# Inverse square root chains of a fused LayerNorm, long-convolution and mixer kernel on GpSimd, with a newly searched issue order

## The chip, the cores and the metric

The kernel runs on one core of a Trainium2 chip. The metric is the device time of one execution in microseconds. Within the core five engines work side by side, each through its own instructions in order: PE (TensorE, matrix products; PEld is its weight load), DVE (VectorE), ACT (ScalarE), POOL (GpSimd) and SP (SyncE, which here only issues DMA transfers). An engine that has to wait holds up everything behind it in its own queue.

## The reference

With S = 2048 positions and D = 512 channels, all in bf16, and `ln` a LayerNorm without weights:

```python
def _layernorm(x, axis=-1, eps=1e-5):
    m = jnp.mean(x, axis=axis, keepdims=True)
    v = jnp.var(x, axis=axis, keepdims=True)
    return (x - m) / jnp.sqrt(v + eps)
...
def _A_ref(q, k, v, shift_k, ssm_k, ssm_D):
    ...                                # k_shift: four shifted copies of k, weighted by shift_k
    kv = k_shift * v
    ...                                # y: causal convolution of kv with ssm_k along S, by FFT
    y = y + kv * ssm_D[None, None, :]
    return q * y
def _B_ref(x, w1, w2, w3, w4):
    h = _gelu(_layernorm(x, axis=-1) @ w1)
    ...                                # g0..g3: quarters of h, shifted by 1, -1, 2, -2 positions
    hs = jnp.concatenate([g0, g1, g2, g3], axis=-1) @ w2
    x1 = x + hs
    h2 = _gelu(_layernorm(x1, axis=-1) @ w3) @ w4      # w3: 512 x 1792, w4: 1792 x 512
    return x1 + h2
x = A_q
h = x + _A_ref(_layernorm(x), A_k, A_v, A_shift_k, A_ssm_k, A_ssm_D)
return h + _B_ref(_layernorm(h), B_w1, B_w2, B_w3, B_w4)
```

Three LayerNorms follow each other: of q, of h, and inside B of the normalised h and then of x1. Each needs an inverse square root of a variance per position.

## The kernel before

**Tiles.** The 2048 positions are 16 tiles `t` of 128 positions; groups `b` = 0 to 3 hold four tiles each. Pairs of tiles are `u` = 0 to 7 (`t` = 2u and 2u+1).

**Stages.** First k is transposed and shifted on PE (`pk`, `psh`), and the convolution runs as two levels of a discrete Fourier transform: `stage_a` makes PSUM tiles `pah` and `pak`, `stage_c` makes `pc`. `product` multiplies the spectra on DVE (L674) and adds the parts (L688, L690). The way back begins with `pg` (L744). Every one of these PSUM tiles has to be evicted to SBUF, by `evac` (L171 on ACT, L173 on DVE).

The h stage follows. `last_level(u)` ends the inverse transform on PE into a PSUM tile `py` (two tiles wide); two instructions scale it by the inverse deviation of q and add 1 (`scaled`, L805 on ACT, L807 on DVE). `gate(u)` multiplies by the centred q on DVE (L812), which is h, and takes the statistics of both tiles (`stats`: bn_stats L620, aggregate L621). When two pairs of a group are there, `rsqrt_h(b)` computes the inverse deviations with all their by-products: two additions to the variance (L824, L825), a first guess by integer arithmetic (L601), two Newton steps of three instructions each (L603 to L605), the negative mean times the factor (`nb`, L827) and a residual weight `rho` (L832, L833). `norm_h(b, i)` then normalises each tile (`hn`, L840 on ACT, L843 on DVE). The normalised tiles are transposed into `xT`: those of b = 0 and 1 by PE (`pt2`, L856, evicted through L171), those of b = 2 and 3 by transposing DMAs on SP's queue (L900).

Then come the products. `gelu_mm("w1", …)` (`pw`, L868; GELU on ACT, L872) makes the hidden state `gT`. `mix(b)` takes shifted columns of `gT` times w2 (`p2`, L945), adds the residual on DVE (`x1`, L951), takes statistics, runs the same inverse square root chain for x1 (L959, L601 to L605, L961), normalises (`xnorm`, L969 on ACT, L972 on DVE), and transposes (PE for b = 0, SP's DMAs, L978, for the rest). Last, for each group, `pw` with w3 and GELU, the product with w4 (`p4`, L1014), the final addition (L1019) and the store. `of` (L1000) prepares the residual.

**Fills.** `warm_up` and `keep` (L880, tile `pv`) are matmuls of zeros that nothing reads.

**The chain.** `newton` yields the seven instructions of guess and Newton steps; `chain` adds each of them to the plan as an operation of DVE of its own. All chains are on DVE; GpSimd has nothing to do behind the front.

**The order.** Nothing is issued when it is called. Each step is recorded in a `Plan` with what it reads and writes and the engines that it may run on. `ISSUE`, a long list of operation numbers that a search left and that is written out in the kernel, then says in which order all of them go to their engines; a letter behind a number (A, V) chooses between ACT and DVE. Costs such as `{"V": 0.58}` or `lat` go into that search alone; they have no effect on the program. Within each engine the list's order is the order of execution.

What the list before says around the h stage: PE runs `pw` of b = 0 and 1, `p2` of t = 4 and 2, `pw` of b = 2, a fill, `p2` of t = 6, `pw` of b = 3, `p2` of t = 8. The eviction of py of u = 0 is shared, one half on DVE and one on ACT; all others are on ACT. SP's eight transposes are t = 8, 11, 10, 9, 15, 14, 12, 13.

## Time and profile before

| | us |
|---|---|
| device time, median of 3 runs | 243.62 (242.0 to 243.78) |
| device time of the profiled execution | 243.34 |
| its span | 241.5 |
| PE busy in the span | 224.7 |
| DVE busy | 161.0 |
| ACT busy | 153.1 |
| POOL busy | 15.4 |

The profile is one execution, recorded instruction by instruction. Its views are a page with the busy time of each engine and the costliest groups of instructions; a timeline; groups of instructions by line within a window; windows with each engine's busy time; and the chain of waits, which is followed back from the last instruction, at each step to what released it, or to the instruction before it on its engine. A line of a group reads: line, engine, operation, tiles, shapes, count, then busy time and mean duration in ns, then the idle time of the engine just before and what ended it. Durations of one DVE, ACT or POOL instruction contain a tail that overlaps with the next one, so that how far an engine advances is read from start to start.

### The profile page before, as it was taken

Reading aid. Unit: us, or ns where it says so; the run is one execution under the profiler, and the core shown is the slowest. Engines: PE = TensorE matmul, PEld = TensorE weight load, DVE = VectorE, ACT = ScalarE, POOL = GpSimd, SP = SyncE. Lnnn points to the kernel's source line nnn. Section 1 sums busy time; section 2 is a strip of 40 time slices with the busy share of each in tenths; the row PEclk is TensorE's granted clock in tenths of the full one; section 3 lists DMA queues with packets and bytes.
Section 4 is the critical chain, followed back from the end, with each engine's and each line's share of the span. In section 5 each row is a group of like instructions: output and inputs, shape, how many; then the busy total and the mean of one; then the engine's idle time right before and its main releaser. Section 6 shows DMA issues by size and latency. Waiting matters only on the chain.

```text
span 241.5 us, 5031 instructions
## 1 busy us (share of the span) xinstructions
PE 224.7 (93%) x2069; PEld 147.6 (61%) x2069; DVE 161.0 (67%) x380; ACT 153.1 (63%) x205; POOL 15.4 (6%) x30
## 2 busy tenths in 40 slices
PE   8899987998899977999969999999999999999994
PEld 7899987897799864574434544444444444444454
DVE  6954999999999997999998899910440044004421
ACT  5788769999979998889657399763036204630000
POOL 2359300000000000000000000000000000000000
PEclk9999999999999999999999999999999999999999
DMA  6998876740000099100640025320002012001111
GB/s 218 391 374 203 168 187 213 174 91 3 0 3 0 20 343 390 39 0 0 88 84 5 1 53 99 61 52 3 10 22 54 0 24 65 0 0 42 46 43 45
DMA packets 22182, 21.82 MB, mean 90 GB/s; under 512 B 11916, under 2 KB 18704, under 8 KB 22160
## 3 DMA queue, kind: packets, MB, share of 16 engines
q1 hardware_dynamic: 21904, 21.37, 32.7%
q8 instruction: 16, 0.26, 0.5%
q10 hardware_dynamic: 256, 0.14, 0.2%
q14 instruction: 6, 0.05, 0.1%
HBM read 13.11 MB, written 2.10 MB: 63 GB/s over the span
## 4 chain that ended last, share of the span: by engine, by line
PE 51%; DVE 25%; DMA 12%; ACT 6%; issue 2%; SPq 1%; DVEq 0%; ACTq 0%
PE pw L868 23%; PE p L1014 20%; DVE kin L674 6%; DMA kin<-in_A_v_dram 5%; PE p L945 4%; DVE bst L620 4%; DVE ab L173 4%; ACT s L171 3%; DMA q_sb<-in_A_q_dram 3%; ACT ab L171 3%; DMA kin<-in_A_k_dram 2%; DVE ab L812 2%; DMA act<-ab 2%; DVE kin L688 1%; DVE bst L624 1%
## 5 line engine op out<-in xcount | busy, mean ns | idle before, releaser
L868 PE MATMUL pw<-act,wts 128*128 128x512 bf16 x288 | 64.0, 379 | 2.5 <-DMA act<-ab 1.9
L872 ACT ACTIVATE ab<-pw 128x512 bf16<-128x512 f32 x56 | 33.0, 596 | 38.4 <-PE pw L868 27.3
L1019 DVE TENSOR_TENSOR wts<-p,wts 128x1024 bf16<-128x1024 f32 (+2 forms) x10 | 10.1, 1012 | 62.0 <-PE p L1014 62.0
L868 PEld LDWEIGHTS <-wts 128*128 128x128 bf16 x288 | 28.0, 98 | 36.3 <-DMA act<-ab 2.4
L1014 PE MATMUL p<-wts,ab 128*128 128x512 bf16 (+1 forms) x238 | 48.9, 366 | 0.0
L1014 PEld LDWEIGHTS <-ab 128*128 128x128 bf16 x238 | 23.3, 98 | 25.3
L542 PE MATMUL pc<-ab,Wc 128*128 128x256 bf16 x128 | 30.7, 282 | 1.4 <-DVE ab L173 1.1
L171 ACT CAST s<-pc 128x1024 bf16<-128x1024 f32 x31 | 29.6, 1044 | 1.4 <-DVE kin L674 1.3
L544 PE MATMUL pc<-ab,Wc 128*128 128x128 bf16 x128 | 29.0, 227 | 0.0
L543 PE MATMUL pc<-ab,Wc 128*128 128x128 bf16 x128 | 28.0, 219 | 0.0
L543 PEld LDWEIGHTS <-Wc 128*128 128x128 bf16 x128 | 19.4, 151 | 1.4 <-issue 1.4
L674 DVE TENSOR_TENSOR kin<-s 128x2048 bf16<-128x2048 bf16 x16 | 19.4, 1221 | 0.6
L542 PEld LDWEIGHTS <-Wc 128*128 128x128 bf16 x128 | 19.4, 151 | 0.3
L544 PEld LDWEIGHTS <-Wc 128*128 128x128 bf16 x128 | 18.2, 142 | 0.0
L477 PE MATMUL psh<-ab 128*128 128x128 bf16 x256 | 15.6, 219 | 0.4 <-DVE kvq L481 0.4
L171 ACT CAST ab<-pah 128x1024 bf16<-128x1024 f32 x13 | 12.8, 1023 | 4.8 <-PE pah L518 4.8
L477 PEld LDWEIGHTS <-ab 128*128 128x128 bf16 x256 | 14.4, 98 | 0.9 <-issue 0.4
L945 PE MATMUL p<-wts,act 128*128 128x512 bf16 x64 | 15.0, 379 | 0.0
L481 DVE TENSOR_TENSOR kvq<-psh,kin 128x1024 bf16<-128x1024 f32 x8 | 9.7, 1218 | 4.8 <-DMA kin<-in_A_v_dram 4.8
L171 ACT CAST ab<-pak 128x1024 bf16<-128x1024 f32 x13 | 12.5, 1061 | 0.0
L951 DVE SCALAR_TENSOR_TENSOR s<-ab,rho,p 128x512 bf16<-128x512 bf16 x16 | 11.5, 739 | 1.2 <-PE p L945 1.1
L1000 DVE SCALAR_TENSOR_TENSOR wts<-s,mq,ab 128x512 f32<-128x512 bf16 x16 | 11.2, 749 | 0.2
(139 smaller groups left out, 316.3 us busy)
## 6 DMA issues: line engine op xcount, KB each, us to landing
wts<-in_B_w_dram SPq DMA_DIRECT2D x2, 1792.0 KB, 11.1
kin<-in_A_k_dram SPq DMA_DIRECT2D x4, 512.0 KB, 5.8
ab<-in_A_ssm_k_dram SPq DMA_DIRECT2D x4, 512.0 KB, 8.6
kin<-in_A_v_dram SPq DMA_DIRECT2D x4, 512.0 KB, 13.6
q_sb<-in_A_q_dram SPq DMA_DIRECT2D x8, 256.0 KB, 6.1
kin<-kvq SPq DMA_DIRECT2D x16, 128.0 KB, 5.1
out_dram<-wts SPq DMA_DIRECT2D x14, 128.0 KB, 2.3
Wc<-ab SPq DMA_DIRECT2D x4, 384.0 KB, 5.3
```

Of the source, the lines that this page charges most:

```text
L171: A.copy(o, src)
L477: T_.matmul(pv[:, g, i, :], lhsT=row(g, 4 * qr + i - j), rhs=dg()[:, 2 * g + cc, j, :], start=(j == 0), stop=(j == 3))
L542: T_.matmul(pv[:, kk], lhsT=W[0], rhs=T[:, :, 2 * k1:2 * k1 + 2, :], start=True, stop=False)
L543: T_.matmul(pv[:, kk, :, 0, :], lhsT=W[1], rhs=T[:, :, 2 * k1 + 1, :], start=False, stop=False)
L544: T_.matmul(pv[:, kk, :, 1, :], lhsT=W[2], rhs=T[:, :, 2 * k1, :], start=False, stop=True)
L674: v(1.13, lambda: V.tensor_tensor(out=prs(), in0=xs(0).unsqueeze(1).to_broadcast([P, 2, 2, 512]), in1=xs(1).unsqueeze(2).to_broadcast([P, ...
L868: T_.matmul(ps[:], lhsT=wt(w)[:, k, m * P:(m + 1) * P], rhs=xT()[:, k, 4 * b * P:(4 * b + 4) * P], start=(k == 0), stop=(k == DC - 1))
L872: add({"A": 0.49}, lambda: A.activation(dst(), X[pkey][:], ACT.Gelu_apprx_tanh), r + [pkey, "gelu"], [key])
L945: T_.matmul(ps[:, i, :], lhsT=gT()[:, m, t + i + 2 + off[m], :], rhs=wt("w2")[:, m, :], start=(m == 0), stop=(m == 3))
L951: v(0.66, lambda t=t, i=i, key=key: V.scalar_tensor_tensor(out=qn()[:, t + i, :], in0=hn()[:, t + i, :], scalar=rho[:, t + i:t + i + 1], i ...
L1000: v(0.66, lambda j=j, i=i, t=t + i: V.scalar_tensor_tensor(out=ofb()[:, j, i], in0=qn()[:, t, :], scalar=mq[:, t:t + 1], in1=hs()[:, t, :] ...
L1014: T_.matmul(ps[:, i, x0:x1], lhsT=g2(b % 2)[:, m, s0:s0 + P], rhs=wt("w4")[:, m, x0:x1], start=(m == 0), stop=(m == FC - 1))
```

## The change

- The chains of h (b = 0 to 3) and of x1 may now go to GpSimd instruction by instruction (letter G in the list). The first guess stays on DVE. GpSimd gets no scalar_tensor_tensor: `stt` makes two instructions of it there. The chain of q stays on DVE (`own=True`).
- In the new list GpSimd has, of the h chains: all of b = 0 and 1 but guess and (b = 0) `nb`; of b = 2 the two additions and everything from the middle of the first Newton step up to `nb`; of b = 3 the two additions and one product of the second step. It has all `rho`. Of x1: nothing of b = 0, and of the others most of what comes behind the first guess. That is 91 instructions more on POOL.
- Both halves of a `py` eviction are one operation of the plan and so on one engine: u = 0 on DVE, the others on ACT. The two operations' reads in `gate` and `of` are named accordingly.
- The second chain of the last x1 group gets a scratch column of its own (`8 if t == 0 else 0`).
- The search's costs are adjusted (`0.6` to `0.615` and so on), which has no effect by itself.
- `ISSUE` is unchanged up to its 255th entry, where in the profile before about 55 us have passed, and new from there. Between there and the first `py`, ACT has 40 evictions instead of 39 and DVE 7 instead of 8; one centring of q moves from DVE to ACT. In the h stage DVE issues all gates and bn_stats of b = 3 ahead of the first normalise of b = 2. PE runs `pw` of b = 2 and of b = 3 directly one behind the other, then `p2` of t = 6; the fills stand ahead. SP's transposes are t = 8, 9, 11, 10, 15, 14, 12, 13. The weights are loaded in the order w2, w4, w1, w3 instead of w1, w4, w2, w3.

```diff
 ISSUE = """
...
-288 197A 290 287 286 125 307 234 294A 297 137 235 289A 291A 305 292 308A 300 302 134 233 232 126 306A 260 242
...
+288 197A 290 287 286 125 307 234 294A 297 137 235 289A 291A 305 292 308A 324 233 232 260 126 306A 274 216V 134
...
     def newton(vv, r, n, b, o=0):
 
         tv = nwt[:, b, o:o + n]
-        yield lambda: V.tensor_scalar(r.bitcast(I32), vv.bitcast(I32), -0.5, 0x5F1FFFF9, op0=MUL, op1=ADD)
+        yield None, lambda: V.tensor_scalar(r.bitcast(I32), vv.bitcast(I32), -0.5, 0x5F1FFFF9, op0=MUL, op1=ADD)
         for a, c in ((-0.703952253, 0.703952253 * 2.38924456), (-0.5, 1.5)):
-            yield lambda a=a: V.scalar_tensor_tensor(out=tv, in0=r, scalar=a, in1=r, op0=MUL, op1=MUL)
-            yield lambda: V.tensor_tensor(out=tv, in0=tv, in1=vv, op=MUL)
-            yield lambda c=c: V.scalar_tensor_tensor(out=r, in0=tv, scalar=c, in1=r, op0=ADD, op1=MUL)
...
+            yield lambda E, a=a: stt(E, out=tv, in0=r, scalar=a, in1=r, op0=MUL, op1=MUL)
+            yield lambda E: E.tensor_tensor(out=tv, in0=tv, in1=vv, op=MUL)
+            yield lambda E, c=c: stt(E, out=r, in0=tv, scalar=c, in1=r, op0=ADD, op1=MUL, same=True)
+
+    def stt(E, out, in0, scalar, in1, op0, op1, same=False):
+        if E is V:
+            V.scalar_tensor_tensor(out=out, in0=in0, scalar=scalar, in1=in1, op0=op0, op1=op1)
         else:
...
+            tmp = in0 if same else out
+            G.tensor_scalar(tmp, in0, scalar, None, op0=op0)
+            G.tensor_tensor(out=out, in0=tmp, in1=in1, op=op1)
+
+    def chain(fns, r, w, own=False):
+        for i, f in enumerate(fns):
+            rr = r if i == 0 else ()
+            if own and not isinstance(f, tuple):
+                v(0.14, lambda f=f: f(V), rr, w, lat=0.22)
+            elif isinstance(f, tuple):
+                v(0.14, f[1], rr, w, lat=0.22)
+            else:
+                two = "stt" in f.__code__.co_names or "stt" in f.__code__.co_freevars
+                add({"V": 0.14, "G": 0.5 if two else 0.24}, lambda e, f=f: f(G if e == "G" else V), rr, w, lat=0.26)
...
-        for i in range(2):
-            def scaled(e, i=i, t=2 * u + i):
+
+        def scaled(e):
+            for i in range(2):
+                t = 2 * u + i
                 if e == "A":
                     A.activation(ysb()[:, u % 4, i], X[key][:, i], ACT.Identity, bias=1.0, scale=rq[:, t:t + 1])
                 else:
                     V.tensor_scalar(ysb()[:, u % 4, i], X[key][:, i], rq[:, t:t + 1], 1.0, op0=MUL, op1=ADD)
-            add({"A": 0.53, "V": 0.6}, scaled, ["W", key, ("rq", 0)], [("y", u % 4, i)])
+
+        add({"A": 1.18, "V": 1.22}, scaled, ["W", key, ("rq", 0)], [("y", u % 4)])
...
-        fns = [lambda: V.tensor_scalar(vh[:, b, :, 0], mvar, EPS, None, op0=ADD),
-               lambda: V.tensor_scalar(vh[:, b, :, 1], mvar, 1.0 + EPS, EPS * EPS, op0=MUL, op1=ADD)]
+        fns = [lambda E: E.tensor_scalar(vh[:, b, :, 0], mvar, EPS, None, op0=ADD),
+               lambda E: E.tensor_scalar(vh[:, b, :, 1], mvar, 1.0 + EPS, EPS * EPS, op0=MUL, op1=ADD)]
         fns += newton(flat(vh[:, b]), flat(rh[:, b]), 8, b)
...
-        v(0.1, lambda: V.tensor_tensor(out=rb, in0=rh[:, b, :, 0], in1=rh[:, b, :, 1], op=MUL), [("rh", b)], [("rho", b)])
...
+        add({"V": 0.11, "G": 0.22}, lambda e: (G if e == "G" else V).tensor_tensor(out=rb, in0=rh[:, b, :, 0], in1=rh[:, b, :, 1], op=MUL), [("rh", b)], [("rho", b)])
```

## The prediction

> **What bounds the kernel now.** I read the profile's page first, its line of busy times:

> ```profile
> PE 224.7 (93%) x2069; PEld 147.6 (61%) x2069; DVE 161.0 (67%) x380; ACT 153.1 (63%) x205; POOL 15.4 (6%) x30
> ```

> PE's 93% says little, because PE is also kept busy with matmuls that compute nothing, and shares of a whole span hide that its stages have different limits. So I cut the span where the work changes, with the view of windows (stretch, its length, busy us of PE, PEld, DVE, ACT, POOL; clock; DMA; GB/s).

> ```profile
> 55.20:93.20 38.00, 32.81 (x451) 30.69 (x449) 37.20 (x57) 36.34 (x40) 0.00 (x0) 1.00 0.26 84
> 93.20:118.40 25.20, 23.31 (x216) 13.72 (x217) 23.10 (x85) 21.86 (x34) 0.00 (x0) 1.00 0.22 75
> 118.40:122.70 4.30, 2.44 (x12) 0.88 (x9) 4.06 (x19) 1.52 (x2) 0.00 (x0) 1.00 0.84 95
> 122.70:238.00 115.30, 115.29 (x565) 54.34 (x566) 50.43 (x138) 48.07 (x79) 0.00 (x0) 1.00 0.16 34
> ```

> Up to 93.2 DVE and ACT are both full, and POOL (GpSimd) has nothing to do in all four. From 93.2 to 118.4 (the h stage) DVE is the fullest. From 122.7 PE works 115.29 of 115.30 us at clock 1.00: nothing that happens off PE there can be felt, unless it makes PE wait anew. So what the change is worth is read at the door of that last stretch. The chain of waits in order of time (start, us, what) shows it:

> ```profile
> 93.27 0.85 PE py L797 x6
> ...
> 118.45 4.22 DMA act<-ab
> 122.67 0.05 issue
> 122.71 3.63 PE pw L868 x16
> 126.34 0.22 PE pv L880 x4
> 126.56 1.73 PE p L945 x8
> 128.29 3.45 PE pw L868 x16
> ```

> I write T for the start of the first py matmul (93.27). PE runs gap-free from T+29.4; that start hangs on the transposing DMAs of group b=2, and these on DVE's h stage. Behind it stand pw of b=2, one p2 product (L945, 1.73), and pw of b=3, which starts at T+35.0.

> **The front of the change: 55 to 93 us.** The two programs issue the same work up to about 55 us. From there to T, DVE gives up two evictions (pak 2 to 1, pg 6 to 5), takes one (s, 0 to 1) and gives up a centre; ACT goes from 39 evictions (its x40 above, less one centre) to 40.

> ```profile
> L171 ACT CAST s<-pc 128x1024 bf16<-128x1024 f32 x23 | 22.2, 1044 | 1.4 <-DVE kin L674 1.3
> L171 ACT CAST ab<-pg 128x1024 bf16<-128x1024 f32 x10 | 9.6, 1038 | 0.2 <-PE pg L744 0.2
> ```

> One more on ACT costs 0.95 (22.2/23 and 9.6/10 give 0.96; the mean of one has its tail in it). ACT's idle time there is 1.4+0.2 = 1.6. If the new order fills all of it, T comes 1.6−0.95 = 0.65 earlier; if none, 0.95 later. DVE, relieved of about 1.2, no longer binds. ACT led DVE by little before and its waits were few, so I take T 0.3 earlier, nearer to the filled end.

> **The h stage, walked.** Sizes are the time that DVE advances for one operation, from the chain of waits:

> ```profile
> 107.37 0.60 DVE ab L812
> ...
> 108.28 0.18 DVE nwt L604
> 108.48 0.17 DVE rh L605
> 108.65 0.09 DVE mvh L621
> 108.74 0.10 DVE nb L827
> 108.85 0.60 DVE bst L620
> 109.45 0.32 DVE ab L843
> ```

> So a gate (L812) advances DVE by 0.60, a bn_stats by 0.60, an aggregate by about 0.10, a normalise (L843) by 0.32, a chain step by 0.20 when it waits for the one before (108.28 to 108.48), and by about 0.10 when other work lies between. Before, 40 chain steps and 8 rho products of the four groups run on DVE. Between the first gate (T+2.5, below) and the last normalise of b=3 (T+27.2) DVE spends 24.7 us; 8 gates, 16 statistics, 16 aggregates and 8 normalises are 4.8+9.6+1.6+2.6 = 18.6, so the chains cost it 6.1. After, DVE keeps 13 steps (7 of them for b=3): 0.6+1.4 = 2.0. It also takes one more normalise (0.32) and three edge copies (about 0.65). The gross gain on DVE is 6.1−2.0−1.0 = 3.1 us. Whether it arrives depends on GpSimd, to which no such chain belonged before.

> ```profile
> 1.05 0.20 POOL masks.py:197 MEMSET ident<- 128x128 bf16 x1
> 1.33 0.29 POOL masks.py:199 TENSOR_SCALAR_AFFINE_SELECT ident<-ident 128x128 bf16<-128x128 bf16 x1
> ...
> 8.02 0.20 POOL L372 TENSOR_TENSOR gt<-CSG,ab 128x4 bf16<-128x4 bf16 x1 [5.52 <-DVE CSG L396]
> 8.16 2.02 POOL L344 IOTA kin<- 128x1024 int32 x2
> 12.12 0.31 POOL L563 TENSOR_TENSOR ab<-ab,dcol 128x2 bf16<-128x2 bf16 x1 [1.94 <-DMA ab<-in_A_ssm_k_dram]
> 13.04 0.18 POOL L407 COPY gt<-kin 128x2 int32<-128x2 int32 x1 [0.61 <-DVE kin L354]
> 13.16 1.84 POOL L411 MEMSET Wc<- 128x1024 uint32 x2
> 17.10 0.20 POOL L563 TENSOR_TENSOR ab<-ab,dcol 128x2 bf16<-128x2 bf16 x1 [2.10 <-DMA ab<-in_A_ssm_k_dram]
> ```

> and on DVE at that time

> ```profile
> 12.09 0.29 DVE L383 TENSOR_SCALAR ab<-ab 128x512 bf16<-128x512 bf16 x1
> ```

> A small operation takes 0.18 to 0.31; the affine select, which waits for the memset, starts 0.08 after its end. Each step of the moved chain waits for the one before, so I put g, start to start, at 0.20+0.08 = 0.28; ends 0.18+0.04 = 0.22 and 0.31+0.08 = 0.39. (A scalar_tensor_tensor becomes two such operations.) The two L563 rows also show 0.31 beside L383, a DVE operation of a normalise's form that ended 0.05 before it, and 0.20 without one: I let GpSimd stand still during gates and normalises, as in that row (the gate has no row; bounds 0 and its 0.60).

> Times from T, in the new order. y of u=0, both halves on DVE from T+1.0 (the py matmuls are 0.85 long): hs at 2.45. Before, DVE had the one half and waited for ACT with the other:

> ```profile
> L807 DVE TENSOR_SCALAR wts<-py,rq 128x512 bf16<-128x512 f32 x1 | 0.8, 751 | 1.6 <-ACT wts L805 1.6
> ```

> That put hs at about 1.6+0.75, T+2.5 with the gaps; pairing the halves gains nothing here, as the second half takes the room of the wait. The other pairs were on ACT as a whole already. Four gates, four statistics, four aggregates: 7.65, the first guess of b=0 (L601, still DVE). Four statistics, four aggregates and a gate: 11.15, while GpSimd's ten operations need 2.8 from 7.8: hidden. nb of b=0, a normalise, the guess of b=1: 11.9. GpSimd now has 13 operations (one rho, ten, two of nb), 3.64, and stands still 0.3+0.6+0.6 for one normalise and two gates: 17.0. DVE reaches the normalise that needs them at 11.9+0.3+6×0.6+0.4 = 16.2 and waits 0.8. Two normalises; then three GpSimd operations (0.84 and 0.5 of standing still) before the guess of b=2: 18.3, two steps: 18.7. A gate and four statistics, 3.0: 21.7; GpSimd needs 8 to 9 operations and a standstill, 3.1 from 18.7: 21.8. nb and an aggregate: hn of t=8 ends at **T+22.3**.

> ```profile
> 113.66 0.81 ACT L840 ACTIVATE ab<-ab,nb,rh 128x512 bf16<-128x512 bf16 x1
> ```

> Before, it ended at 114.47 = T+21.2. So DVE's gain does not reach the first transpose: the new order spends it on all gates and statistics of b=3 ahead of b=2's normalises, to cover GpSimd. What comes earlier is the end: the rest of the stage is three aggregates, hn of t=9 (22.95), three edge copies (23.6), b=3's chain with one operation on GpSimd (1.8: 25.4), three normalises (26.35), against T+27.2 before.

> SP's queue and the landing of its transposes are in two more views:

> ```profile
> L900 SPq DMA_TRANSPOSE act<-ab x8: 1188/1232/1296, 114.5 to 125.1; - x8
> ...
> DMA to landing us min/median/max: 2.4/2.5/4.2
> ```

> One takes up to 1.30. Queued without a pause from T+22.3, the eighth goes out at 22.3+7×1.29 = 31.3, not at 125.1 = T+31.8, and lands 2.5 later: T+33.8. PE gets there in time: p2 of t=4 and t=2 ended at T+27.6 before (the 2.44 of the third window), come some 1.4 later behind the later normalises of b=1, T+29, and pw of b=2 (3.45) ends near 32.5. But the new order puts pw of b=3 directly behind, and the p2 product that stood between (1.73) after it. PE waits 1.3, and the three pieces end at 33.8+3.45+1.73 = 39.0. Before, they ended at 131.74 (128.29+3.45) = T+38.5. So the h stage gives −0.5, less the 0.22 of idle-filling matmuls (pv) that no longer stand in the row: +0.3 us longer.

> **Other edits.** ACT's three centres behind the evictions take 3×0.7 and y of u=1 follows at T+2.2, as before; hs of u=1 is due at 3.65. The load of w1 goes third among the weights:

> ```profile
> wts<-in_B_w_dram SPq DMA_DIRECT2D x2, 1792.0 KB, 11.1
> ```

> At 11.1 us to landing and issued where it was, before T, it is there by T+11; PE needs it only after the transposes of b=0, near T+15: hidden with 4 us of cover. The x chains on GpSimd (b=1 to 3) lie behind PE's full stretch. The first whose transposes PE reads is b=1. PE needs them after five p2, 13 pw and two transposes behind T+39: 5×1.73+13×0.86+1, T+60. Its x1 is done two p2 and a transpose behind T+39 (T+43.4); statistics, three DVE steps and ten GpSimd operations put the chain at T+50, four normalises between ACT's other work at T+53, four transposes and a landing at T+58: hidden by 2 us. [...]

> Sum against the profiled execution's own time, 243.34 (span 241.5; the median of the runs is 243.62, so it stands 0.28 under): −0.3 (front) +0.3 (h stage) +0.2 (held DVE) = +0.2, **243.6 us**.

> **The rivals.** *GpSimd is slow, and DVE stands in line behind it.* DVE is in order; nb of b=0, the normalise of t=7, the guess and nb of b=2 are the four places where it waits for GpSimd, with all gates and statistics queued behind. Some 34 operations lie on that line (10+13+3+8). At g=0.39 that is 34×0.11 less 0.6 of slack = +3.1, 246.7; with T 0.95 late instead of early 247.9. From g=0.36 it is over 1% slower. For it: the fp32 forms have no row on POOL, and 0.31 was seen. Against: two of three tensor rows are at 0.20. Chance 0.33.

> *GpSimd is quick.* At g=0.22 the lines of b=1 and b=2 shorten by 24×0.06 = 1.4, of which 0.8 and 0.5 are DVE's waits; with T 0.65 early the time is 241.9. To pass 1% the first normalises would have to come 2.4 earlier, which the statistics in front of them do not allow: chance 0.12, with an unseen gain in the front counted in.

> *A DMA lands late.* One of the eight took 4.2 instead of 2.5; were it the last, PE would wait 1.7 more (245.3): inside 1%.

> [...]

> That GpSimd gets no chain at all is excluded: its instruction list in the changed program has them, 91 operations more.

> **How the numbers follow.** A change under 1% (2.4 us) can hardly be told from none here. The forecast and the two mild rivals (late DMA, lock) lie within it: 0.55. Slow GpSimd: 0.33 slower. Quick: 0.12 faster. The range runs from 241.9 (quick) to 247.6, just short of both bad ends together (247.9).

> **What would show it.** POOL rows of the chain starting about 0.28 apart; DVE waits named POOL at L854's normalise and at the nb and guess of b=2, about 1.5 us in all; hn of t=8 near T+22.3; SP's eight transposes 1.3 apart; PE waiting for DMA ahead of pw of b=3 and not of b=2, then full to the end. I am wrong if T moves by more than a microsecond, if g is outside 0.22 to 0.39, or if PE waits again behind T+39.

## The result, and the profile after

| | before | changed |
|---|---|---|
| median of 16 runs each, side by side | 243.49 (242.00 to 244.38) | 244.74 (242.74 to 246.00) |
| ratio of the times, 95% interval | | 1.0054 (1.0030 to 1.0078) |
| the profiled execution | 243.34 | 244.29 |
| its span | 241.5 | 242.5 |

The change costs about half a per cent: 1.25 us between the medians, 0.95 between the two profiled executions. The forecast was 243.6, which is +0.26 on the profiled execution. In the changed kernel line numbers of the prediction's steps are higher by 8 to 11 (py L805, bn_stats L628, pw L879, p2 L956, SP's transposes L911).

Busy times first, from the page of the changed kernel:

```profile
PE 226.1 (93%) x2069; PEld 148.0 (61%) x2069; DVE 155.7 (64%) x325; ACT 149.5 (62%) x199; POOL 38.6 (16%) x121
```

DVE has 55 instructions less and POOL 91 more: the chains moved as described. The windows, cut at T, at the end of hn of t=8 and at the last wait of PE (columns as before: stretch, length, busy us of PE, PEld, DVE, ACT, POOL, clock, DMA, GB/s):

```profile
55.20:93.00 37.80, 33.15 (x451) 31.13 (x449) 35.87 (x55) 37.15 (x42) 0.00 (x0) 0.95 0.28 95
93.00:114.60 21.60, 19.48 (x203) 11.57 (x204) 19.93 (x52) 18.41 (x29) 11.03 (x41) 1.00 0.15 58
114.60:127.30 12.70, 10.67 (x50) 4.53 (x48) 10.17 (x44) 7.16 (x13) 1.39 (x6) 1.00 0.49 84
127.30:238.90 111.60, 111.60 (x546) 52.52 (x546) 43.40 (x91) 41.28 (x68) 10.86 (x44) 1.00 0.14 31
```

The last row shows the full stretch unhurt: PE works 111.60 of 111.60 us, with 10.86 us of GpSimd beside it. So the loss lies ahead of 127.30. The clock of the first row, 0.95, is new; it comes back below. The door itself stands in the chain of waits of the changed kernel (start, us, what):

```profile
93.00 0.85 PE py L805 x6
...
124.73 2.43 DMA act<-ab
127.16 0.14 issue
127.30 3.61 PE pw L879 x16
130.91 1.73 PE p L956 x8
132.64 0.45 PE pt L867 x8
```

T moved from 93.27 to 93.00. The three pieces pw of b=2, pw of b=3 and p2 of t=6 end at 132.64 = T+39.64; before, they ended at 131.74 = T+38.47. That is −0.27 and +1.17, together +0.90, and the spans differ by 1.0. PE's timeline shows where the 1.17 comes from. First the changed kernel, then the kernel before (start, us, line, operation, count; in brackets the idle time in front and what ended it):

```profile
121.97 3.63 PE L879 MATMUL pw<-act,wts 128*128 128x512 bf16 x16 [0.33 <-DMA act<-ab]
127.30 3.61 PE L879 MATMUL pw<-act,wts 128*128 128x512 bf16 x16 [1.70 <-DMA act<-ab]
130.75 1.89 PE L956 MATMUL p<-wts,act 128*128 128x512 bf16 x8
```

```profile
122.71 3.63 PE L868 MATMUL pw<-act,wts 128*128 128x512 bf16 x16 [1.88 <-DMA act<-ab]
126.18 0.39 PE L880 MATMUL pv<-zero 128*128 128x128 bf16 x4
126.40 1.89 PE L945 MATMUL p<-wts,act 128*128 128x512 bf16 x8
128.13 3.62 PE L868 MATMUL pw<-act,wts 128*128 128x512 bf16 x16
```

Before, the p2 product lay in the time in which the last four transposes came in, and pw of b=3 found its data ready. Now PE stands idle for 1.70 us there and does the p2 product afterwards. And the last transpose is no earlier than it was. Of the changed kernel's eight (duration of the issue, min/median/max, ns; first and last start):

```profile
L911 SPq DMA_TRANSPOSE act<-ab x8: 1210/1256/2055, 114.7 to 124.7; - x8
...
DMA to landing us min/median/max: 2.4/2.5/4.0
```

The eighth starts at 124.73 = T+31.7; before it was 125.1 = T+31.8. DVE's relief, 3.1 us by the prediction's count, did not move it.

### The profile page after: what moved, and what is told of

Its sections match the earlier page's. It is cut to its first block, busy times and chain, and to the rows that moved or that the text cites. A ratio compares the mean times of both kernels' runs of the same rounds, so it can differ in the third digit from the quotient of the medians.

```text
span 242.5 us, 5068 instructions
## 1 busy us (share of the span) xinstructions
PE 226.1 (93%) x2069; PEld 148.0 (61%) x2069; DVE 155.7 (64%) x325; ACT 149.5 (62%) x199; POOL 38.6 (16%) x121
## 4 chain that ended last, share of the span: by engine, by line
PE 59%; DVE 13%; DMA 10%; ACT 9%; issue 4%; POOL 3%; SPq 1%; DVEq 0%
PE pw L879 24%; PE p L1025 20%; DMA q_sb<-in_A_q_dram 5%; PE p L956 5%; ACT ab L172 4%; PE pc L543 4%; ACT s L172 3%; DMA ab<-in_A_ssm_k_dram 3%; DVE ab L174 2%; PE pc L545 2%; PE pc L544 2%; DVE bst L628 2%; DVE bst L632 2%; DVE kin L682 1%; DVE s L962 1%
## 5 line engine op out<-in xcount | busy, mean ns | idle before, releaser
L879 PE MATMUL pw<-act,wts 128*128 128x512 bf16 x288 | 64.3, 379 | 2.7 <-DMA act<-ab 2.0
L879 PEld LDWEIGHTS <-wts 128*128 128x128 bf16 x288 | 27.9, 98 | 36.6 <-issue 2.9
L543 PE MATMUL pc<-ab,Wc 128*128 128x256 bf16 x128 | 31.4, 287 | 0.3 <-ACT ab L172 0.3
L545 PE MATMUL pc<-ab,Wc 128*128 128x128 bf16 x128 | 29.4, 229 | 0.0
L172 ACT CAST s<-pc 128x1024 bf16<-128x1024 f32 x30 | 28.4, 1054 | 0.7 <-PE pc L545 0.3
L544 PE MATMUL pc<-ab,Wc 128*128 128x128 bf16 x128 | 28.5, 222 | 0.0
L545 PEld LDWEIGHTS <-Wc 128*128 128x128 bf16 x128 | 18.3, 143 | 0.2
L956 PE MATMUL p<-wts,act 128*128 128x512 bf16 x64 | 15.0, 379 | 0.0
L883 ACT ACTIVATE act<-pw 128x512 bf16<-128x512 f32 x16 | 9.2, 610 | 8.0 <-PE pw L879 7.8
L172 ACT CAST ab<-pak 128x1024 bf16<-128x1024 f32 x14 | 13.3, 1093 | 0.0
L835 POOL TENSOR_SCALAR vh<-mvh 128x4 f32<-128x4 f32 x4 | 1.3, 337 | 74.4 <-DVE mvh L629 74.2
## 6 DMA issues: line engine op xcount, KB each, us to landing
wts<-in_B_w_dram SPq DMA_DIRECT2D x2, 1792.0 KB, 10.8
```

The costliest lines, as they stand in the source:

```text
L172: A.copy(o, src)
L543: T_.matmul(pv[:, kk], lhsT=W[0], rhs=T[:, :, 2 * k1:2 * k1 + 2, :], start=True, stop=False)
L544: T_.matmul(pv[:, kk, :, 0, :], lhsT=W[1], rhs=T[:, :, 2 * k1 + 1, :], start=False, stop=False)
L545: T_.matmul(pv[:, kk, :, 1, :], lhsT=W[2], rhs=T[:, :, 2 * k1, :], start=False, stop=True)
L879: T_.matmul(ps[:], lhsT=wt(w)[:, k, m * P:(m + 1) * P], rhs=xT()[:, k, 4 * b * P:(4 * b + 4) * P], start=(k == 0), stop=(k == DC - 1))
L883: add({"A": 0.49}, lambda: A.activation(dst(), X[pkey][:], ACT.Gelu_apprx_tanh), r + [pkey, "gelu"], [key])
```

## The experiments

A ratio is to the kernel before, run on the same chip beside it, with its 95% interval. T and "the door" (the end of those three pieces) come from one profiled execution of each kernel.

**The kernel before once more, and each half of the order alone.** The first kernel is the one before, unchanged.

> The kernel before, unchanged, to have the granted clock of many of its executions. The clock theory (the new order of the front leaves PE so thinly used around 58 to 62 us that its clock is cut there in most executions, and this is what makes the change slower) expects clock 1.000 in nearly all executions here, and one narrow group of times around 243.5. The rival (the clock is cut at random in any version, and the loss sits in the h stage) expects clocks of 0.99 here as often as after the change.

It took 243.28, ratio 1.0009 (0.9991 to 1.0028), at a granted clock of 0.998 or more in eleven of its twelve runs. Its chain of waits at the door:

```profile
119.17 3.44 DMA act<-ab
...
122.65 3.63 PE pw L868 x16
...
130.22 1.46 PE pw L868 x6
```

T was 93.99 and the door at 131.68 = T+37.7, 0.8 earlier than in the first profile, because the transpose that PE waits for landed after 3.44 us and not after 4.22. So the kernel before has no fixed door either: T+38.5 goes with a late landing, and against this second profile the change loses 1.95 and not 1.17.

The second has the old order up to the first py and the new one behind it:

```diff
 ISSUE = """
...
-288 197A 290 287 286 125 307 234 294A 297 137 235 289A 291A 305 292 308A 324 233 232 ...
+288 197A 290 287 286 125 307 234 294A 297 137 235 289A 291A 305 292 308A 300 302 134 ...
...
```

> The changed kernel with the old order up to the first py matmul and the new one behind it. The two traces put the first py at 93.27 before and 93.00 after, and the end of the w1 product of b=3 and the p2 beside it 38.5 us behind it before and 39.6 after. Clock theory: clock 1.000 in nearly all executions, no group of late ones; the h stage's loss of 1.2 remains, so a ratio of 1.004 to 1.006, about 244.7. Rival (h stage harmless, all of the loss from the front): ratio 1.000.

It took 244.77, ratio 1.0062 (1.0039 to 1.0084), at granted clocks of 0.997 to 1.000. T was 92.42 and the door at 131.66 = T+39.2. The third is the reverse, the new front with the old order behind it: chains on DVE, p2 of t=6 ahead of pw of b=3, SP's transposes in their old order.

> The new order up to the first py matmul and the old one behind it, chains on DVE; pairs of y halves on one engine. Clock theory: clocks of 0.99 in most executions, times in two groups as after the change: with clock 1.000 about 1.5 faster than before (242.0), with 0.99 about the time of before or 0.3 over it; median ratio 0.998 to 1.002. Rival (all of the loss from the front): 1.005.

It took 242.98, ratio 0.9987 (0.9964 to 1.0011); T was 92.75 and the door at 131.26 = T+38.5, as in the first profile of the kernel before (a landing of 4.15 again). So the loss sits behind T: about +1.5 us there. The front gives about −0.3, and its interval includes zero. These two make up the change's +1.25.

**GpSimd out of the new order.** The list of the change, with every G of the chains turned into V:

```diff
-453 448 456G 493 486 457G 458 534A 494 459G 460G 461G ...
+453 448 456V 493 486 457V 458 534A 494 459V 460V 461V ...
```

> The changed kernel in its own order, but all chain steps on DVE (no scalar_tensor_tensor is split). If GpSimd's chains bring what the prediction's gross gain says, DVE now has some 27 steps of 0.10 to 0.20 more in the h stage, less the waits on GpSimd that go (about 0.3 in the trace): 2.5 to 4 us slower than after the change, ratio to before 1.012 to 1.02. If GpSimd's latency costs as much as it saves, the time is that of the change, 1.005.

It took 247.41, ratio 1.0173 (1.0145 to 1.0202); the eighth transpose starts at 128.18 = T+34.3 and the door is at T+42.2, both 2.6 later than in the changed kernel. Within this order the move to GpSimd is worth 1.0173 − 1.0054 = 1.2%, 2.9 us, inside what was expected. It is less than the 4.1 (6.1−2.0) by which the prediction relieved DVE of chain steps; its 3.1 also takes off copies and a normalise that stay where they are here. Within this order the chains themselves are no mistake; what the order does with the room is.

**The wait on PE filled again.** In the changed list, p2 of t=6 (operation 647) goes ahead of pw of b=3 (608, 606, 604, 602):

```diff
-... 560 599 564 563 561 565 608 606 604 ... 602 647 639V ...
+... 560 599 564 563 561 565 647 608 606 604 ... 602 639V ...
```

> The changed kernel with one move in PE's order: the p2 product of t=6 (1.73 us) is issued ahead of pw of b=3, as before the change. Theory (the loss sits at PE's wait for the eighth transpose, 1.70 us in the changed kernel's profile, with p2 queued behind it): the wait is filled, PE's full stretch starts 1.5 to 1.7 earlier at the same end of transposes; ratio to the kernel before 0.997 to 1.000, about 1.3 to 1.7 below the changed kernel's 244.7. Rival (PE's clock, or the end of the transposes moving with p2): less than 0.5 below it, ratio 1.003 to 1.006. Rival (p2 is not ready in time and stalls PE itself ahead of pw): nothing gained, and PE waits at p2.

It took 243.67, ratio 1.0026 (1.0003 to 1.0049). That is 0.7 us below the first measurement of the change and 0.3 below its repeat (1.0040, below), less than the 1.3 to 1.7 that were expected; as the intervals overlap, the times alone do not show a gain. From PE's timeline of this kernel:

```profile
128.34 3.61 PE L879 MATMUL pw<-act,wts 128*128 128x512 bf16 x15
...
134.73 0.61 PE L867 MATMUL pt<-ident,act 128*128 128x128 bf16 x8 [0.60 <-ACT act L172]
```

The wait ahead of pw of b=3 is gone and the door is at 131.97 = T+38.4 (T 93.60). But a transposed tile of the next stage is now asked for sooner than ACT evicts it: a new wait of 0.60, which the two runs below with the same p2 move show as well. Door and new wait together, T+39.0, are 0.7 below the changed kernel's T+39.64, so that little more could come of it.

**PE kept busy in the front.** In the changed kernel's profile PE ran at a granted clock of 0.73 and 0.85 from 58 to 66 us, and 13 of its 16 runs had a mean clock of 0.990 to 0.993, while the kernel before has 0.998 to 1.000 in nearly all. Matmuls of zeros, overwritten by what follows, were put in to keep PE busy:

```diff
         def pe():
             pv = psum(ring, key)[:].rearrange("p (g e x) -> p g e x", g=2, e=4)
+            if w == 0 and cc == 1:
+                for _ in range(8):
+                    T_.matmul(X[key][:, 0:P], lhsT=zero[:, 0:P], rhs=zero[:, 0:P], start=True, stop=True)
```

> The changed kernel with eight matmuls of zeros ahead of each of the eight pak products of one half, which keep PE busy in the sparse stretch around 58 to 66 us. Clock theory (the granted clock of 0.73 to 0.85 there is what the mean of the changed kernel loses): clock 1.000 in nearly all executions and 1 to 2 us less than the changed kernel's 244.7. Theory of the wait for the eighth transpose: clock 1.000, but less than 0.5 us of gain, since ACT and DVE and not PE set the start of py; ratio to the kernel before 1.003 to 1.006.

> Both edits, the p2 product ahead of pw of b=3 and the eight matmuls of zeros. If the two causes are separate, the gains add: about 1.6 less than the changed kernel by the wait theory alone (243.1), 2.5 to 3.5 less by both (241.5 to 242.2). If the zeros bring nothing, the same time as with the p2 move alone.

> New front, old order behind it (chains on DVE, p2 ahead of pw), and the eight matmuls of zeros ahead of the pak products of one half. Without the zeros this measured 242.98 at a ratio of 0.9987 with clocks mostly between .991 and .999. Clock theory: clock 1.000 and 0.5 to 1.5 less, ratio 0.993 to 0.997. Otherwise: ratio 0.998 to 1.000, clock 1.000 or not.

| kernel | time | ratio | clocks | T |
|---|---|---|---|---|
| changed, zeros | 245.60 | 1.0094 (1.0065 to 1.0123) | 0.998 to 1.000 | 95.93 |
| changed, zeros and p2 first | 244.91 | 1.0067 (1.0044 to 1.0090) | 0.997 to 1.000 | 95.17 |
| new front, old back, zeros | 244.36 | 1.0056 (1.0033 to 1.0080) | 0.998 to 1.000 but one | 96.71 |

The clock is back in all three and each is slower, by about 1.0 to 1.7 us by the ratios, than its twin without zeros, where the clock theory had expected a gain: the zeros themselves are too long. Each group of eight with its pak product takes PE 0.95 us, all eight 7.6 (57.35 to 64.94, without a pause), where the eight products of the changed kernel took 5.0 with their waits (56.17 to 61.19), and T comes 1.6 to 4 us later. As a test of the clock this dose was too large. Between the first two, p2 first is 0.7 faster again, again with overlapping intervals.

**b=2 ahead of b=3 on DVE.** If DVE's gain never reaches hn of t=8 because the last gate and the four statistics of b=3 stand in front, then b=2's chain has to come back to DVE and go ahead of them. First the changed kernel without any edit, on the same chip, then the edit alone, then with p2 first:

```diff
-... 542 420 436 508G 543V 544G 473A 474 545G 425 570 ...
+... 542 543V 544V 545V 546V 547V 548V 549V 552V 556 553V 557 420 436 508G 473A 474 425 570 ...
...
-... 587V 588V 589G 590V ...
+... 587V 588V 589V 590V ...
```

(542 to 549 are b=2's chain behind its two additions, 552 and 553 the normalises of t=8 and 9, 556 and 557 their transposes, 570 the gate of b=3.)

> The changed kernel without any edit, beside the next two on the same chip. If its loss is a property of its order: ratio to the kernel before 1.003 to 1.008 as first measured, and the eighth transposing DMA lands 33.5 to 35 us behind T with PE waiting 1 to 2 us for it. If the first profile was a chance: a ratio near 1.000, or no such wait.

> The changed kernel with the whole chain of b=2 on DVE, directly behind its first guess, then both normalises of t=8 and 9, and only then the last gate and the statistics of b=3 (nothing else moved, but one step of b=3's chain also on DVE). Theory (the gain of DVE did not reach the first transposed tile because gates and statistics stand ahead of it): hn of t=8 ends 1.3 to 1.7 earlier than in the changed kernel, near T+20; the last transpose, bound by SP's eight in a row and by hn of t=12, lands 0.8 to 1.5 earlier; ratio to the kernel before 1.000 to 1.002 where the changed kernel has about 1.005. Rival (b=3's statistics, now later, hold hn of t=12 to 15): SP pauses before the fifth, the eighth lands as late as before, ratio 1.004 to 1.008.

> The same, and the p2 product of t=6 ahead of pw of b=3 as in the run with that move alone (ratio 1.0026). Theory (both places count, the first transposed tile and the wait that nothing fills): 1 to 1.8 us less than with the p2 move alone, ratio 0.995 to 0.999, the three pieces of PE ending near T+37.5. Rival (PE gets to pw of b=2 no earlier, since p2 of t=4 and 2 end near T+28.7 anyway, or the next evictions bind behind it): ratio 1.001 to 1.003, as with the p2 move alone.

| kernel | time | ratio | T | eighth transpose starts | door |
|---|---|---|---|---|---|
| changed, again | 243.95 | 1.0040 (1.0018 to 1.0062) | 94.34 | T+31.7 | T+39.6 |
| b=2 first | 242.82 | 0.9987 (0.9969 to 1.0004) | 91.72 | T+30.6 | T+38.5 |
| b=2 first and p2 first | 243.29 | 0.9996 (0.9976 to 1.0016) | 94.24 | | T+37.6, and 0.60 behind |

The changed kernel loses again, and its profile repeats the wait of 1.7 and the door at T+39.6, though its T lies 1.3 later than in the first. DVE's timeline in the changed kernel's first profile, around the first transposed tile:

```profile
110.65 0.17 DVE L602 TENSOR_SCALAR rh<-vh 128x8 int32<-128x8 int32 x1
110.85 0.17 DVE L610 SCALAR_TENSOR_TENSOR nwt<-rh 128x8 f32<-128x8 f32 x1
110.94 0.68 DVE L823 TENSOR_TENSOR ab<-wts,q_sb 128x1024 bf16<-128x1024 bf16 x1
111.54 2.46 DVE L628 BATCH_NORM_STATS2 bst<-ab 128x6 f32<-128x512 bf16 x4
113.92 0.19 DVE L610 SCALAR_TENSOR_TENSOR nb<-mvh,rh 128x4 f32<-128x4 f32 x1
...
114.15 0.41 DVE L854 TENSOR_SCALAR ab<-ab,rh,nb 128x512 bf16<-128x512 bf16 x1
```

and with b=2 first:

```profile
109.68 0.17 DVE L602 TENSOR_SCALAR rh<-vh 128x8 int32<-128x8 int32 x1
...
111.09 0.16 DVE L610 SCALAR_TENSOR_TENSOR nb<-mvh,rh 128x4 f32<-128x4 f32 x1
111.29 0.74 DVE L854 TENSOR_SCALAR ab<-ab,rh,nb 128x512 bf16<-128x512 bf16 x2
111.94 0.69 DVE L823 TENSOR_TENSOR ab<-wts,q_sb 128x1024 bf16<-128x1024 bf16 x1
112.54 2.46 DVE L628 BATCH_NORM_STATS2 bst<-ab 128x6 f32<-128x512 bf16 x4
```

From the guess of b=2 to its normalise: 3.50 us with the gate and the statistics in between, 1.61 without. The first transpose goes out at T+20.1 instead of T+21.7, the eighth at T+30.6 instead of T+31.7, PE's wait ahead of pw of b=3 falls from 1.70 to 0.72, and the time falls by 1.1 us against the changed kernel beside it, with intervals that do not meet. The clock does not explain that, as nine of its twelve runs had a cut clock against seven of the changed kernel's. So the loss lies in the order of the h stage. With that, p2 first brings nothing that the times show: of the 0.9 us by which the door comes earlier its new wait takes 0.60.

**The eight pak products split.** One product of the level behind (pc, operation 317) goes ahead of the last two of eight pak products in a row, on the changed kernel and on the one with b=2 first:

```diff
-... 309 304 209A 202 203A 210 264 310 265 317 318V ...
+... 309 304 209A 317 202 203A 210 264 310 265 318V ...
```

> The changed kernel with one product of the level behind (pc of 0,7,0) moved ahead of the last two of the eight pak products on PE, as the old order has one there. Clock theory, second form (executions with a granted clock of .993 or less are slower by about 1 us than those at .998 to 1.000 of the same kernel, because PE runs at half speed for some 3 us behind the eight pak products and starves DVE and ACT): most executions at .997 or more, 0.5 to 1.2 us less than the changed kernel, ratio to the kernel before 0.999 to 1.003 instead of 1.004 to 1.0054. Rival (the low clock only marks executions that are slow for another reason, or the new place of the product costs as much in evictions): ratio 1.003 to 1.007 whatever the clock.

> The same move on top of the kernel with b=2's chain on DVE ahead of b=3's statistics (which measured 242.82, ratio 0.9987, nine of twelve executions at a clock near .993). Clock theory, second form: most at .997 or more, 242.2 to 242.5, ratio 0.995 to 0.9975. Rival: 242.7 to 243.5, ratio 0.998 to 1.001, whatever the clock.

The first took 243.72, ratio 1.0025 (1.0008 to 1.0042), and seven of its twelve runs had a clock of 1.000; its interval overlaps the changed kernel's 1.0040 on the same chip, and reaches into what the rival expected. The second took 242.40, ratio **0.9954 (0.9941 to 0.9967)**, the only version that is clearly faster than both kernels, on five runs; but four of these still had a clock of 0.992 or 0.993. What gives it the last 0.3% is not shown. The front's part in this is taken up below.

## Why the prediction was right and wrong

**The front: right in the mean, in part by luck.** T 0.3 earlier was forecast; the profiled pair has 0.27, and the run with the new front alone about 0.3 by the median. But single executions differ by more: T lies between 92.42 and 93.99 in the three profiles with the old front, and between 91.72 and 94.34 in those with the new one (those with zeros left aside). What the prediction had not seen is the clock. The runs of each kernel with the new front and without zeros, parted by mean granted clock (one run of 245.57 at 0.985, of the new front with the old back, left aside):

| kernel | runs at 0.983 to 0.993: mean | runs at 0.997 to 1.000: mean |
|---|---|---|
| changed | 13: 244.95 | 3: 243.02 |
| changed, again | 7: 244.58 | 5: 243.59 |
| new front, old back | 6: 243.17 | 5: 242.72 |
| changed, pak split | 5: 244.31 | 7: 243.54 |
| b=2 first | 9: 243.00 | 3: 242.33 |
| all V | 4: 247.79 | 2: 246.56 |
| p2 first | 9: 244.05 | 3: 243.42 |
| b=2 first and p2 first | 10: 243.32 | 2: 242.08 |
| b=2 first, pak split | 4: 242.44 | 1: 242.40 |

In all but the last, which has a single run at full clock, the runs with the cut clock take longer on average, by 0.4 to 1.9 us. T in the profiled executions goes the same way: 92.75, 91.72 and 92.33 in the three at 0.998 or more (old back; b=2 first; pak split), 92.99 to 94.34 in the six below. Whether the cut makes these runs long or only marks them is open. The split does not decide it: full clocks went from five of twelve in the changed kernel on the same chip to seven of twelve, which is no clear difference, and the split on the faster version gained as well with four of five clocks cut. With the old front T reached 93.99 at a full clock. The h stage loses without any cut: the old front with the new back had full clocks throughout and a ratio of 1.0062. But in the changed kernel itself the eight runs at full clock average 243.4, about the time of the kernel before (243.25 and 243.49 by the medians beside them). So the clock is not the cause of the loss behind T, and yet how much of the +1.25 goes with it in the changed kernel stays open.

**GpSimd's steps: right.** From POOL's timeline of the changed kernel:

```profile
101.49 0.20 POOL L614 TENSOR_TENSOR nwt<-nwt,rh 128x8 f32<-128x8 f32 x1
101.77 0.20 POOL L605 TENSOR_TENSOR nwt<-nwt,vh 128x8 f32<-128x8 f32 x1
102.06 0.25 POOL L613 TENSOR_SCALAR nwt<-nwt 128x8 f32<-128x8 f32 x1
102.39 0.20 POOL L614 TENSOR_TENSOR rh<-nwt,rh 128x8 f32<-128x8 f32 x1
102.68 0.24 POOL L613 TENSOR_SCALAR nwt<-rh 128x8 f32<-128x8 f32 x1
...
103.91 0.67 POOL L614 TENSOR_TENSOR rh<-nwt,rh 128x8 f32<-128x8 f32 x1
```

Four steps from 101.49 to 102.68 are 0.30 each, where g was put at 0.28; 0.36, from which the slow rival decided, was far. The rival of a quick GpSimd falls with it.

**The lock: on GpSimd's side alone.** The step at 103.91 takes 0.67 instead of 0.20. On DVE's timeline a gate runs at that time:

```profile
103.83 0.69 DVE L823 TENSOR_TENSOR ab<-wts,q_sb 128x1024 bf16<-128x1024 bf16 x1
```

DVE's gates take 0.66 to 0.69 here and 0.68 to 0.69 before, its normalises 0.38 to 0.43 here and 0.38 to 0.41 before. So gates do hold GpSimd here, as the walk assumed without a row: the six POOL steps of the h stage that start within a gate take 0.49 to 0.67 (99.73 to 111.17), the others 0.19 to 0.35. No DVE operation was seen held: no run shows the 0.2 that the sum adds for a held DVE, nor the lock counted among the mild rivals; what the runs show in its place are the durations above. That is so in the other order too, where GpSimd's product starts first:

```profile
106.26 0.20 POOL L605 TENSOR_TENSOR nwt<-nwt,vh 128x8 f32<-128x8 f32 x1
```

```profile
106.32 0.69 DVE L823 TENSOR_TENSOR ab<-wts,q_sb 128x1024 bf16<-128x1024 bf16 x1
```

By the starts that the traces show, the order did not decide who is held: neither of this pair was lengthened, and in the kernel with b=2 first the same product, again 0.06 ahead of a gate (104.98 and 105.04), took 0.79 and the gate 0.68.

**DVE's waits: fewer than forecast.** The view of waits lists, for DVE in the h stage of the changed kernel (line that waits, releaser, us in total, times, longest):

```profile
DVE wts L817 <- PE py L805: 1.2, 1, 1.2
DVE rh L610 <- POOL nwt L605: 0.4, 1, 0.4
```

One wait of 0.4 on GpSimd instead of 1.5 in all: DVE's work in front covers it better than the walk had it. hn of t=8 ended at 114.15+0.41 = 114.56, T+21.6 against T+22.3 forecast. It was still no earlier than before (T+21.2), as the prediction said, and for the reason that it gave: gates and statistics of b=3 first.

**The step that failed: the size of the h-stage term, "+0.3 us longer".** The mechanism was the one named: PE waits for the eighth transpose ahead of pw of b=3, and p2 of t=6 behind it can't fill the wait. Its size was +1.17 in the profiled pair, and +1.95 against the second profile of the kernel before. Two of its terms were off, and so was the time that it was compared with.

First, the spacing of SP's transposes. The sum from hn of t=8 to the door, against the forecast's 39.0: hn 0.74 earlier; 0.13 to the first issue; the eight issues 10.04 instead of 9.03 from first to last, of which one took 2.06 where 1.29 was put for each; landing 2.43 instead of 2.5 and 0.14 more until PE starts; pw 3.61 instead of 3.45. That is −0.74+0.13+1.01−0.07+0.14+0.16 = +0.63, the measured T+39.6. One such long issue stood in the repeat of the kernel before (2.23) and of the change (1.98) as well. The profile from which the 1.30 was read had none, but a landing of 4.2, and its eight took 10.6 from first to last (114.5 to 125.1), though part of that may be waiting for tiles.

Second, the 0.22 for the pv fill was taken off wrongly: T+38.5 was the end of the last piece with the fill ahead of it, so leaving the fill out was already in the comparison. Without that slip the forecast's own terms give +0.4 in all. (As written they add up to 243.54, which the prediction gives as 243.6.)

Third, the old side. T+38.5 was taken for the kernel's door, but hung on that landing of 4.2; with 3.44 it was T+37.7.

**Behind the door: right.** PE is full from 127.30 on, the x chains on GpSimd make no wait, and the load of w1 none either.

**The late DMA** happened (4.0 to landing) and PE did not wait for it, since it wasn't the last. Whether it is free is not shown: the long issue of 2.06, which moved all later ones, comes directly behind it (116.05 and 117.34), and so it does in the repeat (4.01, then 1.98).

## What to carry to other kernels

Room made on an engine is worth what it moves on the path behind that engine: here a gate and four statistics, some three microseconds of DVE, stood ahead of the first of eight queued transposes, and the transposes came no earlier until that tile's chain was put first. When a queue feeds PE tile by tile (here one issue in 1.21 to 2.06 us), keep independent PE work between the consumers of its first and its last items; and take the spacing, and the time that you compare with, from several executions, not from the one at hand.

## What the runs showed of the hardware

```profile
58.00:62.00 4.00, 2.50 (x43) 2.01 (x43) 4.00 (x10) 4.00 (x6) 0.00 (x0) 1.00 0.00 0
62.00:66.00 4.00, 4.00 (x34) 3.63 (x33) 3.71 (x8) 3.34 (x4) 0.00 (x0) 0.57 0.00 0
66.00:70.00 4.00, 4.00 (x54) 4.00 (x52) 2.76 (x3) 3.82 (x5) 0.00 (x0) 1.00 0.02 4
```

```profile
58.00:62.00 4.00, 3.08 (x50) 2.74 (x50) 4.00 (x9) 4.00 (x5) 0.00 (x0) 1.00 0.00 0
62.00:66.00 4.00, 3.98 (x52) 3.90 (x51) 3.77 (x7) 4.00 (x6) 0.00 (x0) 1.00 0.00 0
66.00:70.00 4.00, 4.00 (x54) 4.00 (x53) 3.73 (x5) 3.78 (x5) 0.00 (x0) 1.00 0.01 4
```

In the first, PE was busy for 2.50 of 4 us, with gaps of at most half a microsecond between pak products; then its clock averages 0.57, 34 matmuls run instead of 52, and in the next window DVE, which lives on their output, does 2.76 of 4 instead of 3.73. With 3.08 busy there was no cut in the second. With windows set at the clock's own changes it is sharper: the clock was 0.50 from 62.14 to 65.55 in this kernel, from 59.80 to 63.22 in the changed one, and twice, from 23.95 and from 61.50, in its repeat, for 3.41 us each time. The full-clock stretch ahead of the cut was 54.6 us in the changed kernel and 58.0 in the one with b=2 and p2 first, which is 16 and 17 times 3.41.

One and the same program is cut in some executions and not in others: of the changed kernel's 16 runs, 13 had a mean clock of 0.990 to 0.993 and three 1.000. Why was not shown.

Windows of 3.41 us, counted from the first moment at full clock (5.19 in the changed kernel), tell more than fixed ones. In the window ahead of each of the six cuts around 60 us, PE was busy for 2.11 to 2.17 us (2.11 in the changed kernel, from 56.39); around the same time in the profiles without a cut no window had less than 2.21 (pak split, from 57.28). That is no threshold for PE's busy time, since the kernel before was busy for only 1.53 of the 3.41 us from 120.42, at its door, and kept its full clock, and the early cut in the repeat followed a window with 2.50. The pak products are 64 x 128, those at the door 128 x 512, and several of the pak products waited for an eviction on ACT (0.39, 0.45 and 0.46 us ahead of those at 57.52, 58.43 and 59.36 in the changed kernel); what counts was not tested.
